# The second MLP's first product as a Strassen step over pairs of token tiles, in two PSUM banks in turn

## The chip, the cores and the metric

One core of a Trainium2 chip runs the whole program. The metric is the device time of one execution, in microseconds (us). Beside it there is the span of one profiled execution, which is the time between the first and the last instruction in its trace.

## The reference

```python
def _moe2_ref(x, w_in, w_out, g_ln):          # x: 4608 x 512
    h = x @ w_in                              # 512 x 1024
    h_max = np.max(h, axis=-1, keepdims=True)
    e = np.exp(h - h_max)
    sm = e / (np.sum(e, axis=-1, keepdims=True) + 1e-09)
    solu = h * sm
    mu = np.mean(solu, axis=-1, keepdims=True)
    var = np.mean((solu - mu) ** 2, axis=-1, keepdims=True)
    ln = (solu - mu) / np.sqrt(var + 1e-06) * g_ln
    return (ln @ w_out).astype(np.float32)    # 1024 x 512

x = attention(q, k, v)                        # 8 batches, 8 heads, 576 tokens, head size 64
x = prelu(x @ moe_w_in) @ moe_w_out           # first MLP, 512 x 2048 and 2048 x 512
return _moe2_ref(x, ...)
```

All arrays are float32. The weights reach the kernel as float64 words.

## The kernel before, in words

A float32 product runs as three passes with operands split into a high and a low part (hi·hi, hi·lo, lo·hi), each pass a `128x512` matmul. So every product of a 128 x 128 stationary block with a 128 x 512 moving block is three matmuls.

The program has three stages. Attention comes first, batch by batch. The first MLP follows in two phases of its hidden units (`phase(0, ...)`, `phase(1, ...)`); each phase runs over 9 tiles of 512 positions, and in a tile over 8 chunks of 128 hidden units: 12 matmuls of `pe_h`, the activation on ACT and DVE (`act_g`), 12 matmuls of `pe_o`. Attention of the later batches lies inside phase 0. Phase 1 adds the first phase's partial sums (`load_part`, `finish`), writes the tile to the DRAM array `y_d`, and has spare slots in which `hook1` (L613) runs one step of `prep` at a time: each loads a block of the second MLP's weights, turns it into float32 (`load_w64`, L87 to L103) and splits it into high and low parts (L526 to L538).

The second MLP runs over 36 token tiles of 128 positions (L633 to L641). `load_x` (L148 to L155) brings y in by blocks of 256 KB and splits it on ACT (L154) and DVE (L155). `pe_h2` (L545 to L558) makes h of one token tile: 4 blocks of the 512 inputs x 6 = 24 matmuls into a tile of two PSUM banks; the pool has two such tiles. `norm` (L562 to L578) is a chain of DVE, ACT and POOL instructions on h: maximum (L568), exponential (L569), product and sum (L572), square (L574), power (L576, POOL), scaling (L577). `pe_tr` (L582 to L593) transposes the result by 8 matmuls and splits it (L590 on ACT, L591 on DVE). `pe_out` (L595 to L611) has 24 matmuls with the second weight, a copy on ACT (L603) and the stores. In the loop PE does `pe_tr(t)`, `pe_h2(t + 2)`, `pe_out(t)`, so the norm of a tile lies beside the work of two others.

The order on each engine is not the order of the source alone. A scheduler places the instructions when the program is built, by the program's order and its own estimates; on the chip every engine works through its list in order and waits for what an instruction needs. All transfers are issued by one queue, SP's. Tiles come from pools: a tile takes a slot (`tag`, `bufs`) and the first write into it waits for the last reader of the slot's tile before.

Of the kernel before, what the change touches and what calls it, by code (L numbers as in the profile page):

```python
# [19 lines left out]
def attention_then_two_mlps(  # L20
# [66 lines left out]
    def load_w64(name, src, shape=None, pool=None):  # L87
        """float64 words to float32 in SBUF. The upper word, read as a float32, holds all
        but the last three bits of the exponent where a float32 has its exponent: times
        2**-112 it is right but for those three bits, which a shift brings in; what  # L90
        float32 cannot hold vanishes. The sign and the lower word's bits follow."""
# [6 lines left out]
        w = (pool or wr).tile([P, N], I32, tag="w32", bufs=None if pool else 2, name=f"w32_{name}")  # L98
# [6 lines left out]
    # ------------------------------------------------------------ first MLP  # L105
# [528 lines left out]
    for t in range(NB):  # L634
# [4 lines left out]
        if t + 2 < NB:  # L639
            h2_norm(t + 2)  # L640
# [33 lines left out]
```

## Time and profile before

| | before |
|---|---|
| device time, median of 3 runs | 1389.6 us (1388.19 to 1390.24) |
| span of the profiled execution | 1384.5 us |
| PE busy (matmuls) | 1343.5 us, 97% of the span, 6240 matmuls |
| DVE busy | 794.9 us, 57% |
| ACT busy | 622.4 us, 45% |
| DMA moved | 127.99 MB, 92 GB/s over the span |

The profiled execution's own device time is not on the page; its span is 5.1 us below the median of the runs, and this much lies around the span. PE counts matmuls, PEld the loading of their stationary operands, which runs beside them. A busy PE says that a matmul is under way at that moment, not how fast it goes: that is read from the distance between starts.

### The profile page before, as it was taken

To read this page: it belongs to the slowest core of one execution; us is meant where nothing else is said; L and a number is where in the kernel's file an instruction comes from. 1 tells how busy PE (TensorE), PEld (TensorE's weight loads), DVE (VectorE), ACT (ScalarE), POOL (GpSimd) and SP (SyncE) were. 2 spreads that over 40 slices of the span, in tenths; PEclk is the share of its full clock that TensorE was granted. 3 is DMA by queue.
4 is the path that set the end of the run, shared out by engine and by line. 5 is a ranking of instruction groups with operands and counts; after the bars stand their busy time and mean duration, and the time that the engine had idled before them with its cause. 6 is when DMAs were issued, how large, how long until landed. Compare 5 with 4: busy or idle time off the path is not lost.

```text
span 1384.5 us, 16678 instructions
## 1 busy us (share of the span) xinstructions
PE 1343.5 (97%) x6240; PEld 1091.4 (79%) x6240; DVE 794.9 (57%) x1332; ACT 622.4 (45%) x1169; POOL 45.2 (3%) x64
## 2 busy tenths in 40 slices
PE   3789999999999999999999999999999999999998
PEld 3568888888888888888888888888888888888886
DVE  7999777776856766954432333335454445444442
ACT  4665555544645566753333333323333344343332
POOL 0330000000000000000000000000000000000000
PEclk8799999999999999999999999999999999999999
DMA  9675345443504643432212222122110111111001
GB/s 196 183 210 162 99 133 145 117 140 93 160 35 126 197 152 91 157 117 92 92 46 56 82 91 78 35 72 65 50 54 24 53 54 40 38 47 37 24 23 31
DMA packets 129265, 127.99 MB, mean 92 GB/s; under 512 B 55968, under 2 KB 93856, under 8 KB 129184
## 3 DMA queue, kind: packets, MB, share of 16 engines
q1 hardware_dynamic: 129184, 126.93, 31.9%
q8 instruction: 49, 0.80, 0.2%
q14 instruction: 32, 0.26, 0.1%
HBM read 89.14 MB, written 37.75 MB: 92 GB/s over the span
## 4 chain that ended last, share of the span: by engine, by line
PE 89%; DVE 6%; DMA 2%; issue 2%; ACT 1%; SPq 0%; POOL 0%; POOLq 0%; ACTq 0%
PE acc L195 9%; PE h L166 9%; PE h L165 9%; PE acc L194 9%; PE acc L196 9%; PE h L167 9%; PE h L553 5%; PE h L556 5%; PE h L554 5%; PE o L599 5%; PE o L601 5%; PE o L600 5%; PE tp L589 2%; PE kv L306 2%; PE qtp L363 1%
## 5 line engine op out<-in xcount | busy, mean ns | idle before, releaser
L165 PE MATMUL h<-x,w 128*128 128x512 f32 x576 | 230.5, 400 | 0.0
L166 PE MATMUL h<-x,w 128*128 128x512 f32 x576 | 229.7, 399 | 0.0
L195 PE MATMUL acc<-gg,w 128*128 128x512 f32 x576 | 229.4, 398 | 0.2 <-DVE gg L180 0.2
L194 PE MATMUL acc<-gg,w 128*128 128x512 f32 x576 | 229.2, 398 | 0.0
L167 PE MATMUL h<-x,w 128*128 128x512 f32 x576 | 227.3, 395 | 1.3 <-POOL w L134 1.3
L196 PE MATMUL acc<-gg,w 128*128 128x512 f32 x576 | 226.5, 393 | 0.0
L177 DVE SCALAR_TENSOR_TENSOR g<-rn,nalpha,g 128x512 f32<-128x512 f32 x144 | 108.0, 751 | 186.8 <-ACT g L176 185.7
L175 ACT ACTIVATE rn<-h 128x512 f32<-128x512 f32 x144 | 85.3, 593 | 194.8 <-PE h L167 194.6
L167 PEld LDWEIGHTS h<-x,w 128*128 128x128 f32 x576 | 108.3, 188 | 27.8 <-POOL w L134 2.4
L165 PEld LDWEIGHTS h<-x,w 128*128 128x128 f32 x576 | 108.5, 189 | 26.5 <-ACT x L386 1.2
L194 PEld LDWEIGHTS acc<-gg,w 128*128 128x128 f32 x576 | 108.2, 188 | 26.1 <-ACT gg L179 0.3
L196 PEld LDWEIGHTS acc<-gg,w 128*128 128x128 f32 x576 | 108.2, 188 | 25.7
L166 PEld LDWEIGHTS h<-x,w 128*128 128x128 f32 x576 | 108.5, 188 | 23.8 <-DVE x L387 0.5
L195 PEld LDWEIGHTS acc<-gg,w 128*128 128x128 f32 x576 | 108.3, 188 | 24.0 <-DVE gg L180 0.5
L180 DVE TENSOR_TENSOR gg<-g,gg 128x512 fp32r<-128x512 f32 x144 | 99.6, 691 | 45.6 <-ACT gg L179 44.2
L179 ACT ACTIVATE gg<-g 128x512 fp32r<-128x512 f32 x144 | 90.8, 631 | 76.5 <-DVE g L177 76.4
L553 PE MATMUL h<-wi,x_y 128*128 128x512 f32 x288 | 116.8, 405 | 0.0
L599 PE MATMUL o<-wo,lt 128*128 128x512 f32 x288 | 114.2, 396 | 0.7 <-ACT lt L590 0.7
L601 PE MATMUL o<-wo,lt 128*128 128x512 f32 x288 | 114.0, 396 | 0.6 <-DVE lt L591 0.6
L569 ACT ACTIVATE el<-h,st 128x1024 f32<-128x1024 f32 x36 | 40.3, 1118 | 163.8 <-DVE st L568 163.7
L600 PE MATMUL o<-wo,lt 128*128 128x512 f32 x288 | 113.8, 395 | 0.0
L554 PE MATMUL h<-wi,x_y 128*128 128x512 f32 x288 | 113.0, 392 | 0.0
(111 smaller groups left out, 1875.0 us busy)
## 6 DMA issues: line engine op xcount, KB each, us to landing
xraw<-x_d SPq DMA_DIRECT2D x64, 256.0 KB, 3.2
q<-in_q_dram SPq DMA_DIRECT2D x16, 576.0 KB, 4.8
p_d<-pt SPq DMA_DIRECT2D x36, 256.0 KB, 3.6
part<-p_d SPq DMA_DIRECT2D x36, 256.0 KB, 3.8
y_d<-part SPq DMA_DIRECT2D x36, 256.0 KB, 2.8
xraw_y<-y_d SPq DMA_DIRECT2D x36, 256.0 KB, 3.2
kt<-in_k_dram SPq DMA_DIRECT2D x16, 512.0 KB, 4.2
vt<-in_v_dram SPq DMA_DIRECT2D x64, 128.0 KB, 3.2
```

The lines of the kernel that those rows point to most:

```text
L165: T.matmul(t, wh, x[:, 0, c, :], start=c == 0, stop=False)
L166: T.matmul(t, wh, x[:, 1, c, :], start=False, stop=False)
L167: T.matmul(t, wl, x[:, 0, c, :], start=False, stop=c == KC - 1)
L177: V.scalar_tensor_tensor(g, rn, nalpha[:, fg:fg + 1], g, ALU.mult, ALU.add)
L194: T.matmul(a, wh, g[:, 0, :], start=f == 0, stop=False)
L195: T.matmul(a, wh, g[:, 1, :], start=False, stop=False)
L196: T.matmul(a, wl, g[:, 0, :], start=False, stop=f == FPH - 1)
L553: T.matmul(ts[:, s, :], xh, w[0], start=c == 0, stop=False)
L554: T.matmul(ts[:, s, :], xh, w[1], start=False, stop=False)
L599: T.matmul(o, lt[:, 0, f, :], wo[f][:, 0, :], start=f == 0, stop=False)
L600: T.matmul(o, lt[:, 0, f, :], wo[f][:, 1, :], start=False, stop=False)
L601: T.matmul(o, lt[:, 1, f, :], wo[f][:, 0, :], start=False, stop=f == KF - 1)
```

## The change

Two token tiles of 128 form a pair. The product of a pair, 256 x 512 by 512 x 1024, is cut into 2 x 2 blocks and made by seven products in place of eight (the Winograd form of Strassen's step). Each of the seven has 2 blocks of 128 inputs x 3 passes = 6 matmuls, so that a pair takes 42 matmuls and not 48; there are 18 pairs.

- **PE** writes into two banks in turn, `h2a` and `h2x` (two slots each). A11·B11 goes to `h2a`, A12·B21 to `h2x`, S2·T2 is added onto `h2a`, S1·T1 starts `h2x` anew; then S3·T3 onto `h2a`, S4·B22 onto `h2x`, A22·T4 onto `h2a`. Between them DVE and ACT read the banks: ACT keeps r1, r2 and r5 as copies in SBUF, DVE makes h's quarters as sums (L648, L655, L657), ACT copies the last quarter (L660).
- **y** is loaded by `load_y`, 512 KB in one transfer for a pair (L596), split by seven ACT copies and seven DVE subtractions of `128x256` (L531, L532), with four sums on DVE (L608, L610, L612, L614). The loads of y inside phase 1 are gone.
- **norm** reads h from SBUF. The two token tiles of a pair share one slot of `wp`.
- **The weights** of this product become seven operands of two blocks. `prep` has as many steps as before, with eight subtractions that were not there and six more splits; four operands (B22, T1, T3, T4) are written to DRAM and read back by 1 MB transfers during the last tile of phase 1, into slots of `wp`.
- **The loop** is over pairs: `pe_h2(n + 1, 0)`, `pe_tr(2n)`, `pe_h2(n + 1, 1)`, `pe_tr(2n + 1)`, `pe_h2(n + 1, 2)`, `pe_out(2n)`, `pe_out(2n + 1)`.

```diff
+    STAGED = ("B22", "T1", "T3", "T4")
+    wi_d = {o: dram.tile([P, 2, 2, N], F32, name=f"wi_d_{o}") for o in STAGED}
...
-        w = (pool or wr).tile([P, N], I32, tag="w32", bufs=None if pool else 2, name=f"w32_{name}")
+        w = (pool or wr).tile([P, N], I32, tag="w32", bufs=None if pool else 4, name=f"w32_{name}")
...
             elif ph + 1 < NPH:
                 load_x(x_d[0], (ph + 1, 0), xp, cs)
-            else:
-                load_x(y_d[0], ("y", 0), xp, cs)
...
     w2 = tc.alloc_tile_pool(name="w2", bufs=1, reuse_waits="tile")
-    wi = [w2.tile([P, 2, F2], F32R, name=f"wi{c}") for c in range(KC)]
+    wi = {o: w2.tile([P, 2, 2, N], F32R, name=f"wi_{o}") for o in ("B11", "B21", "T2")}
     wo = [w2.tile([P, 2, C], F32R, name=f"wo{f}") for f in range(KF)]
-    def load_w2i(c, s):
...
+    def put(hi, lo, src):
+        S.activation(hi, src, AF.Copy)
+        V.tensor_tensor(lo, src, f32(hi), ALU.subtract)
+    def put_wi(o, k, src):
+        if o in wi:
+            put(wi[o][:, 0, k, :], wi[o][:, 1, k, :], src)
+        else:
+            t = wr.tile([P, 2, N], F32R, tag="w64", bufs=2, name=f"wis_{o}_{k}")
+            put(t[:, 0, :], t[:, 1, :], src)
+            nc.sync.dma_start(out=wi_d[o][:, :, k, :], in_=f32(t))
+    wb = {}
+    def load_w2i(b, k):
+        r = (2 * (b in ("B21", "B22")) + k) * P
+        c = 2 * N * (b in ("B12", "B22"))
+        wb[b] = load_w64(f"w{b}_{k}", w2i[r:r + P, c:c + 2 * N])
+    def w2i_steps(k):
+        def one():
+            load_w2i("B12", k)
+            load_w2i("B22", k)
+        def two():
+            t3 = wr.tile([P, N], I32, tag="w32", bufs=4, name=f"wT3_{k}")
+            V.tensor_tensor(f32(t3), wb["B22"], wb["B12"], ALU.subtract)
+            put_wi("T3", k, f32(t3))
+            put_wi("B22", k, wb["B22"])
+        def three():
+            load_w2i("B11", k)
+            put_wi("B11", k, wb["B11"])
+            V.tensor_tensor(wb["B12"], wb["B12"], wb["B11"], ALU.subtract)
+            put_wi("T1", k, wb["B12"])
+        def four():
+            load_w2i("B21", k)
+            V.tensor_tensor(wb["B12"], wb["B22"], wb["B12"], ALU.subtract)
+            put_wi("T2", k, wb["B12"])
+            put_wi("B21", k, wb["B21"])
+            V.tensor_tensor(wb["B12"], wb["B21"], wb["B12"], ALU.subtract)
+            put_wi("T4", k, wb["B12"])
+        return [one, two, three, four]
     def load_w2o(f):
         raw = load_w64(f"wo{f}", w2o[f * P:(f + 1) * P, :])
...
         S.activation(wo[f][:, 0, :], raw, AF.Copy)
         V.tensor_tensor(wo[f][:, 1, :], raw, f32(wo[f][:, 0, :]), ALU.subtract)
-    prep = [lambda c=c, s=s: load_w2i(c, s) for c in range(KC) for s in range(2)]
+    prep = w2i_steps(0) + w2i_steps(1)
     prep += [lambda f=f: load_w2o(f) for f in range(KF)]
-    hp = {}
-    def pe_h2(t):
...
-    lns = {}
-    def norm(t):
-        h = hp.pop(t).rearrange("p a n -> p (a n)")
+    ys = {}
+    def load_y(n):
+        raw = wr.tile([P, KC, 2 * P], F32, tag="w64", bufs=2, name=f"yraw_{n}")
+        i, o = divmod(n, 2)
+        nc.sync.dma_start(out=raw, in_=y_d[i][:, :, 2 * o * P:2 * (o + 1) * P])
+        t = xp.tile([P, 7, 2, 2, P], F32R, tag="x", name=f"y_{n}")
+        op = {o: t[:, z] for z, o in enumerate(("A11", "A12", "S2", "S1", "S3", "S4", "A22"))}
+        a = {"A11": raw[:, 0:2, 0:P], "A12": raw[:, 2:4, 0:P],
+             "A21": raw[:, 0:2, P:2 * P], "A22": raw[:, 2:4, P:2 * P]}
+        s = gp.tile([P, 2, P], F32, tag="g", name=f"ys_{n}")
+        def split(o, src):
+            put(op[o][:, 0], op[o][:, 1], src)
+        split("A11", a["A11"])
+        split("A12", a["A12"])
+        V.tensor_tensor(s, a["A21"], a["A22"], ALU.add)
+        split("S1", s)
+        V.tensor_tensor(s, s, a["A11"], ALU.subtract)
+        split("S2", s)
+        V.tensor_tensor(a["A21"], a["A11"], a["A21"], ALU.subtract)
+        split("S3", a["A21"])
+        V.tensor_tensor(s, a["A12"], s, ALU.subtract)
+        split("S4", s)
+        split("A22", a["A22"])
+        ys[n] = op
+    hs, hb = {}, {}
+    def pe_h2(n, part):
+        if part == 0:
+            hb[n] = [psum["h2"].tile([P, N], F32, tag=f"h2{z}", name=f"h2{z}_{n}") for z in "ax"]
+            hs[n] = [gp.tile([P, F2], F32, tag="gg", bufs=3, name=f"hs_{n}_{z}") for z in range(2)]
+        (ba, bx), (ha, hb2) = hb[n][:2], hs[n]
+        op = ys[n]
+        def product(t, a, b, start):
+            for k in range(2):
+                ah, al = op[a][:, 0, k, :], op[a][:, 1, k, :]
+                bh, bl = wi[b][:, 0, k, :], wi[b][:, 1, k, :]
+                go_on = dict(skip_group_check=not start)
+                T.matmul(t, ah, bh, start=start and k == 0, stop=False, **go_on)
+                T.matmul(t, ah, bl, start=False, stop=False, **go_on)
+                T.matmul(t, al, bh, start=False, stop=k == 1, **go_on)
+        def keep(src, z):
+            r = pps[1].tile([P, N], F32, tag="part", name=f"r{z}_{n}")
+            S.activation(r, src, AF.Copy)
+            return r
+        if part == 0:
+            product(ba, "A11", "B11", True)
+            r1 = keep(ba, 1)
+            product(bx, "A12", "B21", True)
+            V.tensor_tensor(ha[:, 0:N], bx, r1, ALU.add)
+            product(ba, "S2", "T2", False)
+            hb[n].append(keep(ba, 2))
+            product(bx, "S1", "T1", True)
+            hb[n].append(keep(bx, 5))
+        elif part == 1:
+            product(ba, "S3", "T3", False)
+            V.tensor_tensor(hb2[:, N:F2], ba, hb[n][3], ALU.add)
+            product(bx, "S4", "B22", False)
+            V.tensor_tensor(ha[:, N:F2], bx, hb[n][2], ALU.add)
+        else:
+            product(ba, "A22", "T4", False)
+            S.activation(hb2[:, 0:N], ba, AF.Copy)
+    lns, els = {}, {}
+    def norm(n, z):
+        t = 2 * n + z
+        h = hs[n][z]
         st = gp.tile([P, 8], F32, tag="st", bufs=4, name=f"st_{t}")
         nm, se, rs, su, sq, rstd = (st[:, z:z + 1] for z in range(6))
-        el = wp.tile([P, 2, F2], F32, tag="w", name=f"el_{t}")
-        e, ln = el[:, 0, :], el[:, 1, :]
+        if z == 0:
+            els[n] = wp.tile([P, 2, F2], F32, tag="w", name=f"el_{n}")
+        e = els[n][:, z, :]
         V.tensor_reduce(nm, h, AX.X, ALU.max, negate=True)
         S.activation(e, h, AF.Exp, bias=nm, accum_out=se)
         V.tensor_scalar_add(se, se, 1e-9)
         V.reciprocal(rs, se)
         V.scalar_tensor_tensor(e, h, rs, e, ALU.mult, ALU.mult, accum_out=su)
         V.tensor_scalar_mul(su, su, -1.0 / F2)
-        S.activation(ln, e, AF.Square, bias=su, accum_out=sq)
+        S.activation(h, e, AF.Square, bias=su, accum_out=sq)
         V.tensor_scalar(sq, sq, 1.0 / F2, 1e-6, ALU.mult, ALU.add)
         G.tensor_tensor(rstd, sq, mhalf, ALU.pow)
-        V.tensor_scalar(ln, e, su, rstd, ALU.add, ALU.mult)
-        lns[t] = ln
+        V.tensor_scalar(e, e, su, rstd, ALU.add, ALU.mult)
+        lns[t] = e
     lts = {}
...
     def first_h2():
         ps_h.release()
         psum["h2"] = tc.alloc_tile_pool(name="ps_h2", bufs=2, space=PSUM, reuse_waits="tile")
-        h2_norm(0)
-    def h2_norm(t):
-        pe_h2(t)
-        norm(t)
-    phase(1, [first_h2, lambda: h2_norm(1)], hook1)
+        load_y(0)
+        pe_h2(0, 0)
+        pe_h2(0, 1)
+        pe_h2(0, 2)
+        norm(0, 0)
+    def second_y():
+        norm(0, 1)
+        load_y(1)
+    def hook2(i, f):
+        hook1(i, f)
+        if i == NTL - 1 and f < len(STAGED):
+            o = ("T1", "T3", "B22", "T4")[f]
+            wi[o] = wp.tile([P, 2, 2, N], F32R, tag="w", name=f"wi_{o}")
+            nc.sync.dma_start(out=f32(wi[o]), in_=wi_d[o])
+    phase(1, [first_h2, second_y], hook2)
     ps_acc.release()
     psum["o"] = tc.alloc_tile_pool(
         name="ps_o", bufs=2, space=PSUM, side="right", reuse_waits="tile"
     )
-    NB = NT // P
-    for t in range(NB):
-        i, o = divmod(t, N // P)
-        if o < 2 and i + 1 < NTL:
-            load_x(y_d[i + 1], ("y", i + 1), xp, (2 * o, 2 * o + 1))
-        pe_tr(t)
-        if t + 2 < NB:
-            h2_norm(t + 2)
-        pe_out(t)
+    NPR = NT // (2 * P)
+    for n in range(NPR):
+        more = n + 1 < NPR
+        if more:
+            pe_h2(n + 1, 0)
+        pe_tr(2 * n)
+        if more:
+            pe_h2(n + 1, 1)
+        pe_tr(2 * n + 1)
+        if more:
+            norm(n + 1, 0)
+            pe_h2(n + 1, 2)
+        pe_out(2 * n)
+        if more:
+            norm(n + 1, 1)
+            if n + 2 < NPR:
+                load_y(n + 2)
+        pe_out(2 * n + 1)
     for pool in (psum["o"], psum["h2"], w2, pps[1], gp, xp, wr, wp):
         pool.release()
```


In the order fences `yraw_6` is pair 6's y as loaded, `ys_6` the tile of its sums, `y_4` the split operands of pair 4, `hs_3_0` h of pair 3's first token tile, `h2a_3` and `h2x_3` its banks, `tp_4` and `lt_4` the transposes of token tile 4 and their split, `el` the result of the norm, `ob` the output of a token tile.

PE before, in the loop of the second MLP, where token tile 6's output ends and tile 7's transposes and tile 9's product begin:

```order
L601 MATMUL o_6_8454<-wo6_4979,lt_6_8402 128x512
L599 MATMUL o_6_8454<-wo7_4980,lt_6_8402 128x512
L600 MATMUL o_6_8454<-wo7_4980,lt_6_8402 128x512
L601 MATMUL o_6_8454<-wo7_4980,lt_6_8402 128x512
L589 MATMUL tp_7_0_8484<-ident_60,el_7_8362 128x128 x4
L589 MATMUL tp_7_1_8491<-ident_60,el_7_8362 128x128 x4
L553 MATMUL h2_9_8498<-wi0_4969,x_y_2_8223 128x512
L554 MATMUL h2_9_8498<-wi0_4969,x_y_2_8223 128x512
```

PE after, in the loop, at the end of pair 3's S1·T1 and the start of its S3·T3:

```order
L635 MATMUL h2x_3_8342<-wi_T1_7619,y_3_8292 128x512
L636 MATMUL h2x_3_8342<-wi_T1_7619,y_3_8292 128x512
L637 MATMUL h2x_3_8342<-wi_T1_7619,y_3_8292 128x512
L693 MATMUL tp_4_0_8377<-ident_60,el_2_8232 128x128 x4
L693 MATMUL tp_4_1_8384<-ident_60,el_2_8232 128x128 x4
L635 MATMUL h2a_3_8341<-wi_T3_7654,y_3_8292 128x512
L636 MATMUL h2a_3_8341<-wi_T3_7654,y_3_8292 128x512
L637 MATMUL h2a_3_8341<-wi_T3_7654,y_3_8292 128x512
```

The eight transposes of a token tile now stand inside the pair's seven products, between S1·T1 and S3·T3, and no longer between an output product and a whole h.

DVE before, in the same loop, one token tile's norm between two transposes' splits:

```order
L591 TENSOR_TENSOR lt_7_8483<-tp_7_0_8484,lt_7_8483 128x512
L591 TENSOR_TENSOR lt_7_8483<-tp_7_1_8491,lt_7_8483 128x512
L568 TENSOR_REDUCE st_9_8523<-h2_9_8498 128x1
L570 TENSOR_SCALAR st_9_8523<-st_9_8523 128x1
L571 RECIPROCAL st_9_8523<-st_9_8523 128x1
L572 SCALAR_TENSOR_TENSOR el_9_8524,st_9_8523<-h2_9_8498,st_9_8523,el_9_8524 128x1024
L573 TENSOR_SCALAR st_9_8523<-st_9_8523 128x1
L575 TENSOR_SCALAR st_9_8523<-st_9_8523 128x1
L577 TENSOR_SCALAR el_9_8524<-el_9_8524,st_9_8523 128x1024
L591 TENSOR_TENSOR lt_8_8573<-tp_8_0_8574,lt_8_8573 128x512
L591 TENSOR_TENSOR lt_8_8573<-tp_8_1_8581,lt_8_8573 128x512
```

DVE after, around the first sum of pair 3 (L648):

```order
L677 TENSOR_SCALAR st_5_8279<-st_5_8279 128x1
L614 TENSOR_TENSOR ys_4_8482<-yraw_4_8479,ys_4_8482 128x256
L679 TENSOR_SCALAR st_5_8279<-st_5_8279 128x1
L681 TENSOR_SCALAR el_2_8232<-el_2_8232,st_5_8279 128x1024
L532 TENSOR_TENSOR y_4_8481<-ys_4_8482,y_4_8481 128x256
L608 TENSOR_TENSOR ys_6_8860<-yraw_6_8857 128x256
L612 TENSOR_TENSOR yraw_6_8857<-yraw_6_8857 128x2x128
L648 TENSOR_TENSOR hs_3_0_8343<-h2x_3_8342,r1_3_8351 128x512
L695 TENSOR_TENSOR lt_4_8376<-tp_4_0_8377,lt_4_8376 128x512
L695 TENSOR_TENSOR lt_4_8376<-tp_4_1_8384,lt_4_8376 128x512
L655 TENSOR_TENSOR hs_3_1_8344<-h2a_3_8341,r5_3_8374 128x512
L657 TENSOR_TENSOR hs_3_0_8343<-h2x_3_8342,r2_3_8366 128x512
L672 TENSOR_REDUCE st_6_8420<-hs_3_0_8343 128x1
```

The sums for pair 6's y, L608 and L612, stand directly ahead of L648, which reads pair 3's bank, and behind pair 4's last sum, L614.

SP before, in the loop's first tiles:

```order
L610 DMA out_0_dram<-ob_0_7968 96x512
L610 DMA out_0_dram<-ob_0_7968 32x512
L153 DMA xraw_y_2_2_8313<-y_d2_86 128x512
L153 DMA xraw_y_2_3_8317<-y_d2_86 128x512
L610 DMA out_0_dram<-ob_1_8057 64x512 x2
```

SP after, in the loop:

```order
L714 DMA out_0_dram<-ob_2_8275 32x512
L714 DMA out_0_dram<-ob_2_8275 96x512
L596 DMA yraw_6_8857<-y_d3_87 128x4x256
L714 DMA out_0_dram<-ob_3_8337 96x512
L714 DMA out_0_dram<-ob_3_8337 32x512
L714 DMA out_0_dram<-ob_4_8464 64x512 x2
```

The load of pair 6's y, one transfer for 256 positions, stands between the stores of token tiles 2 and 3; its slot is that of `yraw_4`.

## Rows read from the trace of the kernel before

**Rows 1.** The page, part 1: busy time, share of the span and instructions.

```profile
PE 1343.5 (97%) x6240; PEld 1091.4 (79%) x6240; DVE 794.9 (57%) x1332; ACT 622.4 (45%) x1169; POOL 45.2 (3%) x64
```

**Rows 2.** The page, part 4: the chain that ended last, by engine.

```profile
PE 89%; DVE 6%; DMA 2%; issue 2%; ACT 1%; SPq 0%; POOL 0%; POOLq 0%; ACTq 0%
```

**Rows 3.** Waits of PE: engine line waited for, us, times, longest us.

```profile
PE o L599 <- ACT lt L590: 0.7, 2, 0.3
PE o L601 <- DVE lt L591: 0.6, 1, 0.6
```

**Rows 4.** Windows: PE, PEld, DVE, ACT, POOL busy (instructions), clock, DMA, GB/s.

```profile
640.00:700.00 60.00, 60.00 (x259) 48.27 (x258) 20.43 (x30) 19.80 (x35) 0.00 (x0) 1.00 0.21 67
...
580.00:600.00 20.00, 20.00 (x88) 16.07 (x87) 19.48 (x34) 16.07 (x29) 0.00 (x0) 1.00 0.75 232
...
1196.09:1220.20 24.11, 24.11 (x115) 19.70 (x113) 11.50 (x22) 9.09 (x18) 1.09 (x2) 1.00 0.17 45
```

**Rows 5.** Timeline of the second MLP: start us, us, engine, operation, idle before.

```profile
1200.06 0.39 PE L553 MATMUL h<-wi,x_y 128*128 128x512 f32 x1
...
1201.46 0.39 PE L553 MATMUL h<-wi,x_y 128*128 128x512 f32 x1
...
1205.14 0.15 DVE L570 TENSOR_SCALAR st<-st 128x1 f32<-128x1 f32 x1 [1.33 <-ACT el L569]
...
1206.85 0.15 DVE L573 TENSOR_SCALAR st<-st 128x1 f32<-128x1 f32 x1
...
1208.32 0.15 DVE L575 TENSOR_SCALAR st<-st 128x1 f32<-128x1 f32 x1 [1.31 <-ACT el L574]
...
1209.20 0.81 DVE L577 TENSOR_SCALAR el<-el,st 128x1024 f32<-128x1024 f32 x1 [0.73 <-POOL st L576]
...
1209.92 1.28 DVE L591 TENSOR_TENSOR lt<-tp,lt 128x512 fp32r<-128x512 f32 x2
```

**Rows 6.** Chain of waits around the second MLP's token tile: start us, us, what.

```profile
1196.09 0.87 PE tp L589 x8
```

**Rows 7.** Groups by form: shapes, count | busy us, mean ns | idle before.

```profile
L568 DVE TENSOR_REDUCE st<-h 128x1 f32<-128x1024 f32 x36 | 44.1, 1224 | 106.8 <-PE h L556 106.8
...
L572 DVE SCALAR_TENSOR_TENSOR el<-h,st,el 128x1024 f32<-128x1024 f32 x36 | 46.2, 1284 | 1.2
...
L577 DVE TENSOR_SCALAR el<-el,st 128x1024 f32<-128x1024 f32 x36 | 29.2, 812 | 26.4 <-POOL st L576 26.4
...
L591 DVE TENSOR_TENSOR lt<-tp,lt 128x512 fp32r<-128x512 f32 x72 | 46.1, 681 | 6.2 <-ACT lt L590 6.2
...
L590 ACT ACTIVATE lt<-tp 128x512 fp32r<-128x512 f32 x72 | 39.0, 599 | 2.4 <-PE tp L589 2.4
...
L569 ACT ACTIVATE el<-h,st 128x1024 f32<-128x1024 f32 x36 | 40.3, 1118 | 163.8 <-DVE st L568 163.7
...
L269 DVE TENSOR_TENSOR mx<-mx,kt 128x256 f32<-128x256 f32 x32 | 14.5, 453 | 0.7
...
L323 DVE TENSOR_TENSOR kk<-kvF,kk 128x256 fp32r<-128x256 f32 x16 | 7.8, 487 | 2.4 <-ACT kk L322 2.4
...
L215 DVE TENSOR_TENSOR part<-acc,part 128x512 f32<-128x512 f32 x36 | 23.7, 682 | 15.7 <-PE acc L196 11.7 <-DMA xraw<-x_d 4.0
```

**Rows 8.** DMA issues: names, queue, count, KB each, median us to landing.

```profile
xraw_y<-y_d SPq DMA_DIRECT2D x36, 256.0 KB, 3.2
...
kt<-in_k_dram SPq DMA_DIRECT2D x16, 512.0 KB, 4.2
...
w_wi<-in_moe_w_in_dram SPq DMA_DIRECT2D x8, 512.0 KB, 3.9
```

**Rows 9.** The tile kt: its transfers from issue to landing.

```profile
DMA to landing us min/median/max: 3.8/4.1/5.6
```

**Rows 10.** Timeline of PE at the end: the two last output products' waits.

```profile
1366.06 0.50 PE L599 MATMUL o<-wo,lt 128*128 128x512 f32 x1 [0.35 <-ACT lt L590]
...
1367.36 0.50 PE L601 MATMUL o<-wo,lt 128*128 128x512 f32 x1 [0.57 <-DVE lt L591]
```

More of the change, by code (lines that the diff above doesn't have):

```diff
@@ L522, in attention_then_two_mlps @@
     w2 = tc.alloc_tile_pool(name="w2", bufs=1, reuse_waits="tile")
-    wi = [w2.tile([P, 2, F2], F32R, name=f"wi{c}") for c in range(KC)]
+    wi = {o: w2.tile([P, 2, 2, N], F32R, name=f"wi_{o}") for o in ("B11", "B21", "T2")}
     wo = [w2.tile([P, 2, C], F32R, name=f"wo{f}") for f in range(KF)]
-    def load_w2i(c, s):
-        raw = load_w64(
-            f"wi{c}_{s}", w2i[c * P:(c + 1) * P, 2 * s * N:2 * (s + 1) * N]
-        )
-        hi = wi[c][:, 0, s * N:(s + 1) * N]
-        S.activation(hi, raw, AF.Copy)
-        V.tensor_tensor(wi[c][:, 1, s * N:(s + 1) * N], raw, f32(hi), ALU.subtract)
+    def put(hi, lo, src):
[35 more added lines that the diff above has]
+        return [one, two, three, four]
     def load_w2o(f):
@@ L538, in load_w2o @@
         V.tensor_tensor(wo[f][:, 1, :], raw, f32(wo[f][:, 0, :]), ALU.subtract)
-    prep = [lambda c=c, s=s: load_w2i(c, s) for c in range(KC) for s in range(2)]
+    prep = w2i_steps(0) + w2i_steps(1)
     prep += [lambda f=f: load_w2o(f) for f in range(KF)]
-    hp = {}
-    def pe_h2(t):
-        i, o = divmod(t, N // P)
-        x = xs["y", i]
-        ts = psum["h2"].tile([P, 2, N], F32, tag="h2", name=f"h2_{t}")
-        for c in range(KC):
-            xh, xl = (x[:, s, c, o * P:(o + 1) * P] for s in range(2))
-            for s in range(2):
-                w = [wi[c][:, z, s * N:(s + 1) * N] for z in range(2)]
-                T.matmul(ts[:, s, :], xh, w[0], start=c == 0, stop=False)
-                T.matmul(ts[:, s, :], xh, w[1], start=False, stop=False)
-            for s in range(2):
-                T.matmul(ts[:, s, :], xl, wi[c][:, 0, s * N:(s + 1) * N],
-                         start=False, stop=c == KC - 1)
-        hp[t] = ts
@@ L632, in attention_then_two_mlps @@
     )
-    NB = NT // P
-    for t in range(NB):
-        i, o = divmod(t, N // P)
-        if o < 2 and i + 1 < NTL:
-            load_x(y_d[i + 1], ("y", i + 1), xp, (2 * o, 2 * o + 1))
-        pe_tr(t)
-        if t + 2 < NB:
-            h2_norm(t + 2)
-        pe_out(t)
+    NPR = NT // (2 * P)
[16 more added lines that the diff above has]
+        pe_out(2 * n + 1)
     for pool in (psum["o"], psum["h2"], w2, pps[1], gp, xp, wr, wp):
```

## The prediction

> **What bounds the kernel now.** The first view is the table of busy times [rows 1]: PE is busy for 97% of the span and no other engine for more than 57%. The chain that ended last says the same [rows 2]: 89% of it are PE's own instructions. So I ask two things of every stage: does PE wait for anything, and does it run at its best rate while it is busy. The list of PE's waits answers the first. Behind attention it has almost nothing left; in the second MLP there are 0.7 us for the split of the transposes by ACT (L590) and 0.6 us for that by DVE (L591) [rows 3], all at the very end of the program [rows 10]. The windows by stage answer the second [rows 4]: in the first MLP, in the crowded stretch where the weights are prepared, and in the second MLP PE is busy for the whole window at a granted clock of 1.00, that is at 2.4 GHz. The timeline gives the rate [rows 5]: the matmul of L553 that starts at 1200.06 and the one at 1201.46 are six apart, so a `128x512` matmul costs 1.40 / 6 = 0.233 us. Two token tiles together take 24.11 us [rows 4]; two rounds of eight transposes at 0.87 us [rows 6] and 96 matmuls at 0.2330 us make 24.1. Nothing is hidden in the second MLP: a matmul taken from there shortens the program by its spacing, unless something else becomes later than PE.
>
> **What the change removes.** 18 pairs lose 6 matmuls each: 108 x 0.2330 = 25.2 us. The transposes, the output products and the number of stationary loads per matmul are as before, so I keep 0.233 as the price of every matmul that stays. The Trainium skill, "TensorE: Matmul & The Clock Gate", section "Back-to-back issue gap", gives about 131 ns for a sustained matmul of 512 columns; by it the saving would be 14 us. The rows here are against it.
>
> **What it adds on PE's path: the lap of a pair.** A pair now has 90 matmuls and two rounds of transposes: 90 x 0.233 + 2 x 0.87 = 22.7 us, against 24.1. This is the time in which all else of a pair must be done.
>
> By its sum neither engine beside PE is the bound. DVE has the run counted below, 12.95 us, and another two sums and two splits at 0.68, one scaling at 0.81 and three instructions of `128x256`, about 18 us in all [rows 7]. ACT has ten copies of `128x512` at 0.60, four passes over `128x1024` at 1.12 and seven copies of `128x256` that are no longer than 0.60 each: at most some 15 us [rows 7]. But DVE works in order, and there is a ring through it. L648 reads the bank in which S1·T1 is to start, so PE's S1·T1 waits for L648. Ahead of L648 the order has L608 and L612, which wait for the load of y three pairs ahead. That load waits for its slot, which L614 frees, at the end of the DVE run that starts with L657. And L657 needs S4·B22, three products behind L648. Around the ring:
>
> - PE from L648 to the end of S4·B22: 18 x 0.233 + 0.87 = 5.07 us, and 0.24 for the handing over at both ends. This is an estimate: from L575's end at 1208.47 to L577's start at 1209.20 there are 0.73 us for two handings and POOL's power itself [rows 5], so one handing is well under 0.3.
> - DVE from L657 to L614: L657 and two splits L695 at 0.68 each, two maxima at 1.22, two products at 1.28, one scaling at 0.81, six splits at 0.49, one sum at 0.45 and seven small ones of 0.15, in all 12.95 us [rows 7], the `128x256` splits taken from the row of L323, the sum from L269, the small ones from L570 and L573 [rows 5]. Neighbours that don't need each other overlap by about 0.09 (L577 at 1209.20 lasts 0.81, the next begins at 1209.92), those that do don't (from L570 at 1205.14 to L573 at 1206.85). With some 15 of 21 independent that is -1.3. The wait for POOL's power, those 0.73 us, has one split of 0.49 in it now; I count up to 0.5 for it and for other holes. I take 12.2; with no overlap it is 13.4, with all overlapping 11.7.
> - The load: 512 KB in runs of 1 KB. Loads of k of that size and run took 3.8 to 5.6 us, median 4.1 [rows 9]; the weights' 512 KB 3.9, y's 256 KB now 3.2 [rows 8]. The second MLP's stage is quiet (DMA share 0.17, against 0.75 at 580 us [rows 4]), so I take 3.9; the ends are 3.2 and 5.6.
> - L608 and L612 at 0.45, L648 at 0.68: 1.59 us.
>
> The sum is 5.07 + 0.24 + 12.2 + 3.9 + 1.59 = 23.0 us, 0.3 more than PE's lap. The order has this ring from pair 3 to pair 14 (y ends with pair 17), so it costs 12 x 0.3 = 3.6 us. At best it is 21.8 and costs nothing; with 13.4 and 3.9 it is 24.2, and 12 x 1.5 = 18 us are lost. The Trainium skill, "DMA: Bandwidth & Descriptors", section "Anatomy of one DMA", has 2.0 us and the bytes at 436 GB/s, for GpSimd's path: 3.2 us for this load, with which the ring would lie under PE's lap and cost nothing. The measured 256 KB load here takes that long already, so I don't go by it.
>
> **The other turns of the banks.** After each product the other bank's product covers its reading: 6 x 0.233 = 1.40 us, against ACT's copy of 0.60 [rows 7] and two handings. r1 and r2 are copied under A12·B21 and S1·T1. They cost nothing; if ACT's order put a long instruction (an exponential of 1.1 us) ahead of a copy, a turn could lose some 0.3 us. Bounds for all turns: 0 to 5 us, I take 0.
>
> **Where the two MLPs meet.** The first pairs need y of the tile before, the weights from DRAM (1 MB each, issued during the last tile's first four chunks of 24 matmuls, 5.6 us each) and r1's slot, which waits for a store of the first MLP's last tile. The order mixes the last chunks' matmuls with the first pairs' products, so each step has other work beside it, but several short waits are likely. The trace of before has nothing like it; the bounds are 0 (all is covered, as now) and 6 us (a load of y and its splits once in the open). I take 2.
>
> **Preparing the weights.** Eight subtractions and six more splits at 0.68 us [rows 7] are some 10 us more of DVE, just where DVE is busiest: 19.48 of 20 us at 580 us [rows 4]. PE is two chunks, some 11 us, ahead of it, and does not wait there now. I take 0.5; bounds 0 and 3. The 8 MB of writing and reading back (eight times 512 KB, four times 1 MB) has cover in this phase: its DMA share is 0.21 at 640 us [rows 4].
>
> **The end.** Before, the last two token tiles have their splits in the open: 0.35 and 0.57 us for the first of them [rows 10], 1.3 us for both [rows 3]. After, the transposes of both last tiles stand one behind the other, and the second's cover part of the first's splits: -0.7; bounds -1.5 and 0.3.
>
> **Sum.** -25.2 + 3.6 + 0 + 2 + 0.5 - 0.7 = -19.8 us. The profiled span is 1384.5; it becomes 1364.7. The median of the runs lies 5.1 above that span, so the time is 1369.8, and I say 1370.
>
> **Rivals.**
> - *The ring is under PE's lap.* The load takes 3.6 or less, or DVE overlaps more: -25.2 + 2 + 0.5 - 0.7 gives 1366; with the smaller bounds 1363. For it: y's 256 KB landed in 3.2. Against: every 512 KB row is at 3.8 or more.
> - *The ring is well above it.* ACT's halves of the splits and exponentials stand in DVE's path more than I allow, and the run is 12.7 to 13.4 us. The lap is then 23.5 to 24.2, which costs 12 x 0.8 to 1.5 in place of 3.6: 1376 to 1384; with a run of 14 it is 1391. For it: DVE waited 6.2 us for ACT at L591 and 26.4 for POOL at L577 in the trace of before. Against: two tiles' norms are now interleaved and fill each other's waits.
> - *Every turn of a bank waits.* If the sums and copies are not under the other bank's product, 0.6 us of ACT's copy at two turns of each of 18 pairs costs 22 us: 1388 without the ring's share, 1391 with it, no change. Against: 1.40 us of cover.
> - *Slower.* The same ring with loads of 5.6, the longest of the row, in every lap: 5.07 + 0.24 + 12.6 + 5.6 + 1.59 = 25.1, 2.4 over PE's lap, 12 x 2.4 = 29 us in place of 3.6, more than is saved: 1395. It decides from a lap of about 24.7, where the 12 pairs lose what all 18 gain; from 24.9 the time is above 1392.4. Against: that load was measured in the crowded start.
> - *Matmuls cheaper than their spacing.* By the skill's 131 ns the time would be 1370 + 11 = 1381. As a mechanism: six matmuls fewer, with something else setting the pace. The rows show 0.233 without a gap.
>
> **Chances.** My forecast with small errors (1366 to 1375) 0.55, the ring under the lap 0.17, well above it 0.18 (a third of this beyond 1382), every turn waiting 0.04, slower 0.05, cheaper matmuls 0.01. A measurement of this kernel can tell 0.2%, 2.8 us, from no change: faster is below 1386.8, slower above 1392.4. Faster 0.90, within 0.05, slower 0.05. The range that holds 8 in 10 is 1363 to 1382; the likeliest case's own is 1366 to 1375.
>
> **What would show it.** In the changed kernel's profile PE has 6240 - 108 = 6132 matmuls. In the second MLP's window a pair takes 22.7 to 23.2 us and the spacing is still 0.233. In the list of PE's waits the largest entry of this stage is the first matmul line of a product (L635) for DVE's L648, about 0.3 us and some 12 times, and before L608 DVE waits for the load of y. If that wait is missing and the lap is 22.7, my run of DVE is too long; if it is 1 us or more, it is too short. Waits for ACT's copies (L641) at each turn would show the third rival. I would be wrong altogether if the spacing rose with the new order of stationary and moving operands, or if phase 1 had new waits of PE.

## The result and the profile after

The changed kernel takes 1365.89 us (median, 1363.29 to 1369.75) against 1388.89 us before, a ratio of 0.984 (95% interval 0.982 to 0.986); timed a second time it took 1365.72 us, a ratio of 0.983 (0.981 to 0.984). The prediction was 1370 with a range of 1363 to 1382. The direction, the size and the range hold. The step that I thought the likeliest, a ring that costs 0.3 us a lap, did not come: the time is that of the rival "the ring is under PE's lap" (1366, chance 0.17), and just below the likeliest case's own 1366 to 1375. One of the ten runs of the kernel with an eighth product, below, took 1524.52 us at a mean granted clock of 0.82 and is left out of its ratio; all others had 0.99.

The page's first part after answers to [rows 1]: 6132 matmuls, 108 fewer, and DVE and ACT 83 and 63 us busier.

```profile
PE 1319.7 (97%) x6132; PEld 1070.1 (78%) x6132; DVE 877.5 (64%) x1562; ACT 685.1 (50%) x1337; POOL 45.9 (3%) x64
```

The list of PE's waits after answers to [rows 3]; these are all that begin behind attention, and none of them is for L648:

```profile
PE acc L200 <- ACT pt L217: 1.4, 1, 1.4
...
PE h2a L635 <- ACT r L641: 0.5, 1, 0.5
...
PE o L703 <- ACT lt L694: 0.3, 1, 0.3
```

PE's timeline after, the first transposes of two pairs that follow each other (start us, us, engine, operation):

```profile
1146.80 1.03 PE L693 MATMUL tp<-ident,el 128*128 128x128 f32 x8
...
1169.53 1.03 PE L693 MATMUL tp<-ident,el 128*128 128x128 f32 x8
```

The lap is 22.73 us, where two token tiles took 24.11 [rows 4]. The fifteen whole laps in the trace are 22.73 or 22.74, but for two of 22.77 and 22.78. Where the whole difference lies is seen from two points that PE passes in both kernels: the first MLP's matmuls number 1008, in the middle of phase 0, and 3312, with 144 matmuls of the first MLP still to come (counted from 0; the expectations below call the first one the 1008th). These are the rows of PE's timeline, first of before, then of after:

```profile
357.23 0.40 PE L165 MATMUL h<-x,w 128*128 128x512 f32 x1
```

```profile
910.06 0.39 PE L165 MATMUL h<-x,w 128*128 128x512 f32 x1
```

```profile
359.82 0.39 PE L171 MATMUL h<-x,w 128*128 128x512 f32 x1
```

```profile
914.87 0.40 PE L171 MATMUL h<-x,w 128*128 128x512 f32 x1
```

| part of the span, us | before | before, second trace | after | after, second trace |
|---|---|---|---|---|
| to matmul 1008 | 357.23 | 359.05 | 359.82 | 359.04 |
| from there to matmul 3312 | 552.83 | 552.83 | 555.05 | 553.38 |
| from there to the end | 474.44 | 474.42 | 449.43 | 449.18 |
| span | 1384.5 | 1386.3 | 1364.3 | 1361.6 |
| device time of that run | not given | 1388.29 | 1366.02 | 1363.41 |

The second MLP, with the place where it meets the first, is 25.1 us shorter. The weights' preparation in the middle part costs 0.5 to 2.2 us. The first part moves by 1.8 us between two traces of the same kernel, so its difference says nothing of the change.

### The profile page after: what moved, and what is told of

It reads as the page before. It is cut to its first block, busy times and chain, and to the rows that moved or that the text cites. A ratio compares the mean times of both kernels' runs of the same rounds, so it can differ in the third digit from the quotient of the medians.

```text
span 1364.3 us, 16866 instructions
## 1 busy us (share of the span) xinstructions
PE 1319.7 (97%) x6132; PEld 1070.1 (78%) x6132; DVE 877.5 (64%) x1562; ACT 685.1 (50%) x1337; POOL 45.9 (3%) x64
## 4 chain that ended last, share of the span: by engine, by line
PE 84%; DVE 7%; DMA 5%; ACT 2%; issue 1%; SPq 1%; POOL 0%; ACTq 0%; DVEq 0%
PE h L171 8%; PE h L173 8%; PE h L172 8%; PE acc L200 8%; PE acc L202 8%; PE acc L201 8%; PE o L703 5%; PE o L704 5%; PE o L705 5%; PE h2a L635 2%; PE h2a L637 2%; PE h2a L636 2%; PE tp L693 2%; PE kv L312 2%; PE h2x L637 2%; PE h2x L636 2%
## 5 line engine op out<-in xcount | busy, mean ns | idle before, releaser
L183 DVE SCALAR_TENSOR_TENSOR g<-rn,nalpha,g 128x512 f32<-128x512 f32 x144 | 108.2, 752 | 178.1 <-ACT g L182 177.2
L185 ACT ACTIVATE gg<-g 128x512 fp32r<-128x512 f32 x144 | 90.7, 631 | 78.9 <-DVE g L183 78.6
L186 DVE TENSOR_TENSOR gg<-g,gg 128x512 fp32r<-128x512 f32 x144 | 99.6, 692 | 45.2 <-ACT gg L185 43.9
L171 PEld LDWEIGHTS h<-x,w 128*128 128x128 f32 x576 | 108.4, 188 | 25.1 <-ACT x L392 1.6
L182 ACT ACTIVATE g<-h 128x512 f32<-128x512 f32 x144 | 85.3, 592 | 0.0
L695 DVE TENSOR_TENSOR lt<-tp,lt 128x512 fp32r<-128x512 f32 x72 | 46.4, 684 | 51.0 <-ACT lt L694 51.0
L161 DVE TENSOR_TENSOR x<-xraw,x 128x512 fp32r<-128x512 f32 x64 | 43.2, 688 | 37.6 <-ACT x L160 37.5
```

The lines of the kernel that those rows point to most:

```text
L171: T.matmul(t, wh, x[:, 0, c, :], start=c == 0, stop=False)
L183: V.scalar_tensor_tensor(g, rn, nalpha[:, fg:fg + 1], g, ALU.mult, ALU.add)
L185: S.activation(gg[:, 0, :], g, AF.Copy)
L186: V.tensor_tensor(gg[:, 1, :], g, f32(gg[:, 0, :]), ALU.subtract)
```

## The experiments

**An eighth product.** The spacing of the matmuls was to be tested as the price.

```diff
             product(ba, "A22", "T4", False)
+            product(ba, "A22", "T4", False)
```

> Edit: A22·T4 is added a second time, so a pair has 48 matmuls again, as before the change, in the changed kernel's order (h's last quarter then holds that product twice). Theory (the gain is the number of matmuls times their spacing, 0.233 us, and nothing else of the change costs PE anything in the loop): 18 x 6 x 0.2333 = 25.2 us more than the changed kernel's 1365.9, that is 1391, some 2 us above the kernel before, and a lap of 24.1 us per pair. Rival (a matmul is worth less than its spacing, about 0.131 us): 14 us more, 1380. Rival (the lap is set by DVE's ring, not by PE): less than 25 us, as the first part of the added time fills a gap.

It took 1390.63 us, 24.7 more than the changed kernel's 1365.89; against before, timed in the same round, the ratio is 1.0013 (1.0003 to 1.0023). Two pairs' transposes in its timeline of PE:

```profile
1134.52 1.03 PE L694 MATMUL tp<-ident,el 128*128 128x128 f32 x8
...
1158.66 1.03 PE L694 MATMUL tp<-ident,el 128*128 128x128 f32 x8
```

The lap is 24.14 us. The order in two banks, the larger loads and the added work of ACT and DVE gain nothing by themselves: with as many matmuls the kernel is some 2 us above the one before, and the gain is the matmuls' spacing.

**Two products on one bank, then two on the other.**

```diff
-            product(bx, "A12", "B21", True)
-            V.tensor_tensor(ha[:, 0:N], bx, r1, ALU.add)
             product(ba, "S2", "T2", False)
             hb[n].append(keep(ba, 2))
+            product(bx, "A12", "B21", True)
+            V.tensor_tensor(ha[:, 0:N], bx, r1, ALU.add)
```

> Edit: S2·T2 goes ahead of A12·B21, so that two products on the first bank and then two on the second follow each other and no longer take turns. Theory (the turns hide the reading of a bank): PE waits at two places of each pair, for ACT's copy r1 (0.60 and two handings, about 0.85 us) and for DVE's sum L648 (0.68 and two handings, about 0.95 us): 18 x 1.8 = 32 us more, 1398, slower than the kernel before. Rival (the copies are not on PE's path in either order): 1366, no change. The number of matmuls is the same in both.

It took 1369.48 us (ratio to before 0.986, 0.985 to 0.988): 3.6 us more than the changed kernel and not 32. My theory of this edit fell by its size, and the timeline of PE, PEld, ACT and DVE says why:

```profile
1143.68 0.40 PE L637 MATMUL h2a<-wi_B,y 128*128 128x512 f32 x1
...
1143.92 0.40 PE L635 MATMUL h2x<-wi_B,y 128*128 128x512 f32 x1
...
1144.12 0.60 ACT L641 ACTIVATE r<-h2a 128x512 f32<-128x512 f32 x1 [0.80 <-PE h2a L637]
...
1144.77 0.19 PEld L635 LDWEIGHTS h2a<-wi_T,y 128*128 128x128 f32 x1 [0.20 <-ACT r L641]
...
1144.85 0.42 PE L635 MATMUL h2a<-wi_T,y 128*128 128x512 f32 x1
...
1146.49 0.40 PE L637 MATMUL h2x<-wi_B,y 128*128 128x512 f32 x1
...
1146.73 1.03 PE L693 MATMUL tp<-ident,el 128*128 128x128 f32 x8
...
1147.00 0.69 DVE L650 TENSOR_TENSOR hs<-h2x,r 128x512 f32<-128x512 f32 x1 [1.05 <-PE h2x L637]
...
1147.74 0.50 PE L635 MATMUL h2x<-wi_T,y 128*128 128x512 f32 x1
```

The scheduler did not keep the order of the source. It put four matmuls of A12·B21 between the two products on the first bank, its last two behind S2·T2, and the transposes ahead of S1·T1. The rows give the price of both turns. On the first bank the last matmul starts at 1143.68, ACT's copy runs from 1144.12, the load of the next product's stationary operand waits 0.20 us for it, and that product starts at 1144.85. That is 1.17 us from start to start, 0.94 more than a matmul's spacing, and the four matmuls in between cover nearly all of it. On the second bank the last matmul starts at 1146.49, DVE's sum (L650 here, L648 in the changed kernel) ends at 1147.69, and S1·T1 starts at 1147.74: 1.25 us, 1.02 more than a spacing, of which the eight transposes cover about three quarters. The rest, some 0.25 us, stops PE in every lap and makes most of the 0.28 us by which the lap, 23.01 us, is longer. So the prices in my theory, 0.85 and 0.95, were nearly right; that they would lie in the open was not. In the changed kernel a whole product of 1.40 us covers either turn.

**Six matmuls fewer, with and without the ring.** The ring had not shown itself, so I took PE's lap below it. The second kernel leaves out the same product and gives y as loaded a third slot.

```diff
-            product(ba, "A22", "T4", False)
```

> Edit: A22·T4 is left out, so a pair has 36 matmuls (h's last quarter lacks that product). PE's lap falls by 1.40 to 21.3 us. Theory (the ring through L614, the load of y, L608, L648 and three products is real and takes about 22.3 us by the changed kernel's trace, 0.4 under PE's lap): from pair 3 to pair 14 the lap is 22.3, PE waits about 1.0 us for L648 in each, and the time is 1365.9 - 25.2 + 12 = 1353. Rival (there is no such ring): the whole 25.2 us are gained, 1341, with no wait of PE.

```diff
-            product(ba, "A22", "T4", False)
...
-        raw = wr.tile([P, KC, 2 * P], F32, tag="w64", bufs=2, name=f"yraw_{n}")
+        pool, tag, bufs = (w2, "yraw", 1) if n % 3 == 2 else (wr, "w64", 2)
+        raw = pool.tile([P, KC, 2 * P], F32, tag=tag, bufs=bufs, name=f"yraw_{n}")
```

> Edit: as the one without A22·T4, and y as loaded has three slots in place of two, so that its load no longer waits for L614 of the pair before; DVE's order is the same. Theory (the ring, broken here): PE's lap of 21.3 us in every pair, 1365.9 - 25.2 = 1341, and no wait for L648. Rival (what holds the lap at 22.3 or more without A22·T4 is DVE's amount of work, not the ring): 1353 as without the third slot.

With two slots it took 1345.00 us (ratio 0.969, 0.967 to 0.970), with three 1339.79 (0.965, 0.964 to 0.966). The largest of PE's waits with two slots:

```profile
PE h2x L635 <- DVE hs L648: 2.6, 9, 0.5
```

The timeline around one of them, from one L657 to the next:

```profile
1094.52 0.69 DVE L657 TENSOR_TENSOR hs<-h2x,r 128x512 f32<-128x512 f32 x1 [0.68 <-PE h2x L637]
...
1105.55 0.57 SPq L596 DMA_DIRECT2D yraw<-y_d  x1
...
1109.42 0.43 DVE L608 TENSOR_TENSOR ys<-yraw 128x256 f32<-128x256 f32 x1 [1.17 <-DMA yraw<-y_d]
...
1110.23 0.68 DVE L648 TENSOR_TENSOR hs<-h2x,r 128x512 f32<-128x512 f32 x1
...
1110.97 0.50 PE L635 MATMUL h2x<-wi_T,y 128*128 128x512 f32 x1 [0.24 <-DVE hs L648]
...
1116.35 0.69 DVE L657 TENSOR_TENSOR hs<-h2x,r 128x512 f32<-128x512 f32 x1 [0.68 <-PE h2x L637]
```

With three slots there is no wait for that sum in the list, and DVE, with the same order, no longer waits for the load; the laps are 21.33 us, which is PE's own time. So DVE's amount of work does not hold the lap. With two they lie between 21.65 and 22.06 as long as y is loaded, with twelve pauses of PE ahead of S1·T1, and are 21.33 behind that. So the ring is real, it is the load's slot that closes it, and here it takes about 21.84 us on average: 12 x 0.51 = 6.1 us, of which the times show 5.2. In the rows it is 11.03 us from L657 to the load's issue, 3.87 to L608, 1.49 to the end of L648 and 5.44 to the next L657, 21.83 in all. My 1353 had it at 22.3, from the changed kernel's trace, where the first part is 11.66; in this kernel the scheduler ordered DVE's list another way (L614, for one, stands one instruction earlier).

**Both kernels again.**

> Edit: none, the kernel before once more, for a second trace. Theory (the first trace of it was a run with a quick start): the 1008th matmul of the first MLP comes between 357 and 360 us, likely later than the first trace's 357.2, with a span of 1384 to 1387 and a device time 1.7 us above the span. Rival (the change delays the start): 357 us again.

> Edit: none, the changed kernel once more, for a second trace and more times. Theory (the part up to the first matmuls of phase 0's third tile is the same code in both kernels and differs from run to run by what its first loads take; PE's wait for ACT's copies of the partial sums near 508 us comes from the longer preparation of the weights): the time of the 1008th matmul of the first MLP lies anywhere from 357 to 360 us, the wait near 508 us is there again with 0.2 to 1.5 us, and the median is 1364 to 1367. Rival (the start is made slower by the change): 359 to 360 us again.

The times and parts are in the table above. The part to matmul 1008 is 359.05 us in the second trace of before and 359.04 in that of after, and 358.0 to 361.4 in the other changed kernels: it varies by more than the first traces of the two kernels differ, so the quick start of the first trace of before was chance, as far as two traces of before can show. The device time of the second trace of before is 2.0 us above its span, not 1.7. The wait near 508 us is 1.39 us in the first trace of after and not there in the second, where PE loses some 0.1 us at that place; the other changed kernels lose 0 to 1.35 us there, before has no loss in either trace. My lower bound of 0.2 was too high. What moves it is read from the traces in the step on the weights, below.

**The subtractions on POOL, and another slot for r1 of pair 0.**

```diff
-            V.tensor_tensor(f32(t3), wb["B22"], wb["B12"], ALU.subtract)
+            G.tensor_tensor(f32(t3), wb["B22"], wb["B12"], ALU.subtract)
...
-            r = pps[1].tile([P, N], F32, tag="part", name=f"r{z}_{n}")
+            pool, tag = (gp, "rn") if (n, z) == (0, 1) else (pps[1], "part")
+            r = pool.tile([P, N], F32, tag=tag, name=f"r{z}_{n}")
```

(The other three subtractions of `w2i_steps` in the same way.)

> Edit: the changed kernel with the eight subtractions of the weights' preparation on POOL in place of DVE, and r1 of pair 0 in a slot that does not wait for a store of the first MLP. Theory (the wait near 508 us comes from DVE, whose list has one more subtraction ahead of the activation; the wait near 953 us is r1's slot): both waits gone, 1.4 and 0.5 us less, 1364, at the border of what can be measured. Rival (the wait near 508 us comes from the loads' landing): it stays, 1365.5. Bound on the other side: a subtraction on POOL takes 1.48 us and not 0.69, and what waits for it is later; no PE wait is expected from it.

It took 1367.77 us (ratio 0.985, 0.983 to 0.986), no gain. Neither wait is in its trace; since the one near 508 us is missing in other traces too, this run alone does not settle what causes it. But the list has new ones, here the two largest behind attention:

```profile
PE acc L200 <- DVE part L221: 1.8, 1, 1.8
...
PE h2x L635 <- DVE hs L649: 0.6, 1, 0.6
```

The first lies near 600 us, 10 us after a subtraction on POOL runs beside two splits on DVE:

```profile
591.58 1.67 POOL L575 TENSOR_TENSOR w_wB<-w_wB,w_wB 128x512 f32<-128x512 f32 x1 [4.89 <-DVE w_wB L108]
...
592.02 2.39 DVE L161 TENSOR_TENSOR x<-xraw,x 128x512 fp32r<-128x512 f32 x2
...
599.58 0.66 ACT L105 ACTIVATE w_wo<-w_wo 128x512 f32<-128x512 f32 x1 [4.44 <-DMA w_wo<-in_moe_w_out_dram]
...
600.80 0.69 DVE L186 TENSOR_TENSOR gg<-g,gg 128x512 fp32r<-128x512 f32 x1 [2.12 <-ACT gg L185]
```

Two splits take 2.39 us there, the first of them alone 1.78, where such a one takes 0.69. SP issues the next loads, that of `w_wo` the last of them, when these splits are done. But the longest wait in the chain is ACT's: it stands idle for 4.44 us until `w_wo` has landed, L105 runs at 599.58, and behind it L185, for which DVE's L186 waits 2.12 us; the partial sum L221 behind that frees PE's bank only at 602. In the changed kernel this L185 stands ahead of this L105. So two things work together in these rows, the order that the scheduler found for this kernel and the longer split, which put off the issue of `w_wo` by up to 1.1 us; the run does not separate them. The second wait is one lap of the ring of 23.57 us, with the slowest of this trace's loads of y, 4.9 us to landing where the median is 3.7. I foresaw the longer subtraction, but not what it does to DVE, nor a wait of PE; what the slot of r1 is worth alone was not measured.

**One slot for each bank.**

```diff
-        psum["h2"] = tc.alloc_tile_pool(name="ps_h2", bufs=2, space=PSUM, reuse_waits="tile")
+        psum["h2"] = tc.alloc_tile_pool(name="ps_h2", bufs=1, space=PSUM, reuse_waits="tile")
```

> Edit: one slot in place of two for each of the two banks (two PSUM banks in all, not four); the order of the loop from pair 2 on is the same, only where the two MLPs meet are pairs 0 and 1 no longer mixed. Theory (a pair's first product starts 48 matmuls after the last reading of its bank, so the second slot is not needed in the loop): the lap stays 22.73 us, and the meeting of the two MLPs costs 2 to 8 us more, 1368 to 1374. Rival (PE needs the second slot at every pair): a lap longer by a turn of about 0.9 us, 16 us more, 1382.

It took 1370.62 us (ratio 0.987, 0.985 to 0.988), 4.9 us more than the changed kernel in the same round, and the laps are 22.73 us but for one of 23.09. In the loop two banks are enough. The second pair of slots pays where the MLPs meet, as pairs 0 and 1 are mixed there.

## Why the prediction was right, step by step

- **The matmuls, -25.2.** Right: the lap fell by 1.38 us, and the eighth product brings 24.7 us back. The 131 ns a matmul of the Trainium skill ("TensorE: Matmul & The Clock Gate", "Back-to-back issue gap"), by which 14 us would be won or lost, is not what these runs show; the rival that rested on it is out.
- **The ring, +3.6.** This step failed. The ring exists, but in the changed kernel it is shorter than PE's lap. DVE's and SP's timeline of one lap after, from L657 to L648:

```profile
1150.68 0.69 DVE L657 TENSOR_TENSOR hs<-h2x,r 128x512 f32<-128x512 f32 x1 [0.68 <-PE h2x L637]
...
1161.11 0.82 DVE L681 TENSOR_SCALAR el<-el,st 128x1024 f32<-128x1024 f32 x1 [0.44 <-POOL st L680]
...
1161.90 0.42 DVE L614 TENSOR_TENSOR ys<-yraw,ys 128x256 f32<-128x256 f32 x1
...
1162.34 0.57 SPq L596 DMA_DIRECT2D yraw<-y_d  x1
...
1166.23 0.43 DVE L608 TENSOR_TENSOR ys<-yraw 128x256 f32<-128x256 f32 x1 [0.84 <-DMA yraw<-y_d]
...
1167.03 0.68 DVE L648 TENSOR_TENSOR hs<-h2x,r 128x512 f32<-128x512 f32 x1
...
1168.13 0.39 PE L635 MATMUL h2x<-wi_T,y 128*128 128x512 f32 x1
```

  From L657 to the load's issue DVE takes 11.66 us, not 12.2; the load takes 3.89 us to L608 (I had 3.9); L608 to the end of L648 1.48 (1.59). With 5.44 from the end of L648 to L657, taken from the trace with six matmuls fewer (1110.91 to 1116.35), that is 22.5 us, 0.2 to 0.3 under the lap. L648 ends at 1167.71, and S1·T1 starts on time at 1168.13. The mis-sized term is DVE's run, and in it the sum of the durations. The 22 that the prediction lists add up to 12.29 us, not to 12.95, and to 12.74 with L614, which the list leaves out. In the trace these 23 instructions have 12.25 us of durations, 17 of the 22 neighbours overlap, by 1.34 us in all (I had 1.3 for 15 of 21), and the idle time between them is 0.72 us (I had 0.5). With 12.29 in place of 12.95 the same working gives 11.5 for the run and 22.3 for the ring (22.7, PE's own lap, with L614), and nothing for its cost: it is my rival "the ring is under PE's lap" at 1366. So the loop of waits was found and its pieces were priced nearly rightly; a slip in one sum put it above the lap. DVE does wait for the load, 13 times and 9.9 us in all, but PE does not see it:

```profile
DVE ys L608 <- DMA yraw<-y_d: 9.9, 13, 1.2
```

- **The other turns, 0.** Right, with 0.94 and 1.02 us for a turn against 1.40. Where the source did not take turns the scheduler put other work under them.
- **Where the MLPs meet, +2, and the end, -0.7.** Together 0.1 us was measured (-25.1 in the whole part, of which -25.2 are matmuls). PE waits 0.50 us for r1; ACT's copies of this kind have 4.5 us of idle time that a store of the first MLP's last tile ends, as I thought of r1's slot. At the end 0.3 us of waits are left of 1.3 [rows 3]. The 2 us were too many.
- **Preparing the weights, +0.5.** Too little in the first trace (2.2, with the wait of 1.39 near 508 us), right in the second (0.5). In the first trace the wait has this chain in its rows: ACT turns a block of the weights into float32 as soon as it has landed (L105), DVE has one subtraction more ahead of an activation (L560 ahead of L183), ACT's split of it (L185) starts late, the copies of the partial sums (L217) stand behind that, and PE waits for a bank. I had looked at how far PE is ahead of the activations, and not at what else stands behind them on ACT.

```profile
504.91 0.67 ACT L105 ACTIVATE w_wB<-w_wB 128x512 f32<-128x512 f32 x1 [0.17 <-DMA w_wB<-in_moe_w_in_dram]
...
507.60 0.69 DVE L560 TENSOR_TENSOR wT<-w_wB,w_wB 128x512 f32<-128x512 f32 x1
...
508.20 0.75 DVE L183 SCALAR_TENSOR_TENSOR g<-rn,nalpha,g 128x512 f32<-128x512 f32 x1
...
508.99 0.63 ACT L185 ACTIVATE gg<-g 128x512 fp32r<-128x512 f32 x1 [1.46 <-DVE g L183]
509.52 1.07 ACT L217 ACTIVATE pt<-acc 128x512 f32<-128x512 f32 x2
...
510.15 0.50 PE L200 MATMUL acc<-gg,w 128*128 128x512 f32 x1 [1.39 <-ACT pt L217]
```

  The second trace has the same chain, without a wait in the list:

```profile
502.46 0.68 ACT L105 ACTIVATE w_wB<-w_wB 128x512 f32<-128x512 f32 x1 [0.20 <-DMA w_wB<-in_moe_w_in_dram]
...
507.71 0.50 PE L200 MATMUL acc<-gg,w 128*128 128x512 f32 x1
```

  From L105 to PE's matmul it is 5.24 us in the first and 5.25 in the second, and 5.24 to 5.26 in each of the six traces in which PE loses time here; in the two of changed kernels without a loss, PE comes 5.5 and 5.6 us behind L105. So what moves the wait from run to run is how late this load lands, seen from PE; the subtraction is 0.60 us of the chain behind it. The kernel with the subtractions on POOL is the one with 5.5: at that distance the chain with L560 on DVE, 5.25, would not have stopped PE either, so the wait that is missing there says nothing of the subtraction. Why the load lands sooner or later, seen from PE, stays open.

- **The base.** I put 5.1 us around the profiled span of before. The runs of which both numbers are known have 1.7 to 2.1. So the profiled execution took about 1386.5 and was quicker than the median, mostly by its start. In the sum this cancels, as 1384.5 and 5.1 make the median of three runs, 1389.6; with a fourth run it is 1388.89. The change itself was to be -19.8 us and is -23.0 and -23.6 in the two rounds; the ring's 3.6 us are about the difference, and what the other steps had wrong nearly cancels.

## What to carry to other kernels

Where PE is busy without a gap at a granted clock of 1.00, as here, a change is worth its matmuls times their spacing, as long as every other loop of waits stays below the new lap; add up each such loop from a trace, slots and loads included, before the next matmuls are taken out, since here only 0.3 us were left until a third slot opened it. Add up a list of terms twice: here a slip of 0.66 us in one sum decided which side of PE's lap the ring was on. One profile's span moves by its start alone (1.8 us between two traces here), so a base comes from several runs. Where a scheduler orders the engines, look at the order before an edit of the source is taken for an experiment.

## What the runs showed of the hardware

After a wait of PE of 2.86 us, in the kernel with one slot, the next matmuls are 0.43 us apart, not 0.233. Its timeline of PE:

```profile
948.94 0.40 PE L202 MATMUL acc<-gg,w 128*128 128x512 f32 x1
952.20 0.80 PE L635 MATMUL h2a<-wi_T,y 128*128 128x512 f32 x1 [2.86 <-ACT r L641]
...
953.64 0.63 PE L635 MATMUL h2a<-wi_T,y 128*128 128x512 f32 x1
954.07 0.63 PE L636 MATMUL h2a<-wi_T,y 128*128 128x512 f32 x1
...
955.95 0.39 PE L635 MATMUL h2x<-wi_T,y 128*128 128x512 f32 x1
956.18 0.40 PE L636 MATMUL h2x<-wi_T,y 128*128 128x512 f32 x1
```

The windows of the same kernel (columns as in [rows 4]) show the granted clock at 0.50, that is 1.2 GHz, for these 3.3 us and at 1.00 ahead of and behind them:

```profile
940.00:949.00 9.00, 9.00 (x41) 7.18 (x39) 8.60 (x23) 3.78 (x10) 0.00 (x0) 1.00 0.29 95
952.20:955.50 3.30, 3.30 (x8) 2.62 (x9) 0.67 (x1) 0.34 (x1) 0.00 (x0) 0.50 0.07 25
956.00:960.00 4.00, 4.00 (x19) 3.21 (x18) 1.03 (x2) 0.60 (x1) 0.00 (x0) 1.00 0.00 0
```

So that wait cost 2.86 us and some 1.5 us more for eight matmuls. The waits in the other kernels, the longest of 1.8 us, were followed by matmuls at the full rate. The other thing that I had not expected is DVE beside POOL: two splits in 2.39 us while POOL's subtraction took 1.67. In that trace a DVE instruction of `128x512` begins during six of POOL's eight subtractions; the six take 1.00 to 1.79 us, where such ones take 0.68 to 0.75 by themselves. Each of them ends 0.55 us behind the subtraction, whenever it began: it is held until POOL is done, rather than slowed. The other way round, the subtraction takes 1.67 us in the five places where such a DVE instruction was under way at its start, and 1.29 or 1.30 in the three where none was. The Trainium skill, "GPSIMD Engine Reference", section "1. Specifications", has the two engines share their ports to SBUF, with contention when a DVE instruction reads two SBUF inputs, as a split does; these rows agree.
